# Row tiles 4 to 7 of an attention output projection in Strassen's form, in a gated attention and token-mixing kernel

## The chip, the cores and the metric

The kernel runs on one core of a Trainium2 chip. The metric is the time of one execution in device microseconds (us). The engines are TensorE (PE in the profile; PEld is its weight load), VectorE (DVE), ScalarE (ACT), GpSimd (POOL) and SyncE (SP), which only issues transfers. Each engine runs its own instructions in their order and waits for others through semaphores.

## What is computed

```python
x = A_x                                              # (1, 2048, 640), 32 heads of 20
g = sigmoid((x * gate_w).sum(-1, keepdims=True))
qkv = (x @ wqkv).reshape(B, S, 3, H, Dh)             # to q, k, v of (B, H, S, Dh)
p = softmax(einsum("bhqd,bhkd->bhqk", q, k) * Dh ** -0.5)
a = einsum("bhqk,bhkd->bhqd", p, v) -> (B, S, D) @ wo
h = layernorm(x);  u = gelu(einsum("bsd,sf->bdf", h, w1) + b1)
b = transpose(einsum("bdf,fs->bds", u, w2) + b2)
out = g * a + (1 - g) * b
```

All of it is float32. The change touches only the last product, `@ wo`, and the steps that prepare its operands.

## The kernel before

The order of every engine's instructions is the order of the code. First come the q, k and v projections and the token MLP, whose gated result is left in DRAM (`y_d`). Then a loop over 16 pairs of heads (p = 0 to 15, 32 steps each) does scores, exponentials (ACT) and the product with v (PE, `pv_flush`), and for later pairs the row maxima (DVE). `pv_evac` (L1036) copies each result from PSUM and stores the unnormalised rows of the output in `o_d` and the softmax denominators in `l_d`. The denominators of heads 0 to 27 are inverted inside the loop and stored in `r_d`. Those of the last four heads come only after the loop: `last_load` (L1019, tile `rl_last`), `last_recip` (L1025, on DVE, then a store to `rc_d` by ACT's queue), and `l_rest` (L1146), which reads `rc_d` back spread over rows.

**The projection at the end.** The attention output is transposed: 640 channels in five chunks of 128 rows, 2048 positions. Chunks 0 to 3 are loaded in eight groups of 256 positions (`e_load`, tiles `ore` for the values and `rbe` for the inverse denominators, two buffers of each); chunk 4, which holds the last heads, in four groups of 512 (`l_load`, `l_rest`, tiles `orl` and `rbl`). A group is multiplied and split in two: a high part in the fast float32 format of PE and the remainder (`o_high`, L1109, and `o_low`, L1119; `ohe`, `ole`, `ohl`, `oll`). Groups 0 to 2 of the chunks 0 to 3 are done by POOL in the last pair of the loop; the others by DVE (multiply, subtract) and ACT (copy) while the projection runs.

A row tile is 128 positions by 640 outputs, computed in two halves of 320 columns. Each product of two split operands takes three matmuls (high by high, high by low, low by high):

```python
        passes = []
        for k in cs:
            (oh, ol), n, i = (o_hl[t // 2], 2, k) if k < NC - 1 else (l_hl[t // 4], 4, 0)
            cc = slice((t % n) * P, (t % n + 1) * P)
            passes += [(oh[:, i, cc], woh[k]), (oh[:, i, cc], wol[k]), (ol[:, i, cc], woh[k])]
        mms = [(i, c) for i in range(len(passes)) for c in halves]
```

So chunks 0 to 3 of a tile cost 4 x 3 x 2 = 24 matmuls of 128x320 (`a_tile`, L1263), and chunk 4 costs 6. Tile 0 and half of tile 1 are computed inside the last pair of the loop; the other half of tile 1 follows the loop, then tiles 2 to 7 with chunks 0 to 3, and then tiles 8 to 15 with all five chunks, each followed by chunk 4 of the tile eight below it (loop at L1317). PSUM banks go round in the order `two`, `one1`/`one0`, `s`, `s3`/`pv`. The evacuation (L1290) is one DVE instruction per half: it scales by the gate and adds to the tile `oy`, loaded from `y_d` by `y_load`; it then holds the output.

Transfers of SP and ACT share eight numbered semaphores, taken in turn: a transfer is issued only after the earlier one of the same number has landed.

Of the kernel before, what the change touches and what calls it, by code (L numbers as in the profile page):

```python
# [24 lines left out]
HALF = D // 2  # L25
# [6 lines left out]
def gated_mix(ctx, tc, xT, x, wqk, wv0, wv1, wo, w1, w1t, b1, w2, b2, out):  # L32
    nc = tc.nc
# [735 lines left out]
    evacs = []  # L769
# [323 lines left out]
    tys = {}  # L1093
# [28 lines left out]
    def e_load(q):  # L1122
        o_load(q, slice(0, (NC - 1) * P), NC - 1, 256, "e", 2)

    def e_high(q, pool, eng=nc.scalar):
        o_hl[q] = o_high(q, NC - 1, 256, "e", 2, pool, eng)

    def e_low(q, eng=nc.vector):
        o_low(q, "e", o_hl[q], eng)

    L0 = (H - LAST) * DH - (NC - 1) * P

    l_raw = []

    def l_tiles():
        l_raw[:] = [ap.tile([P, 4, 512], F32, name=f"{n}l") for n in ("or", "rb")]
        for q in range(4):
            o_raw[q, "l"] = [t[:, q:q + 1] for t in l_raw]

    def l_load(q):  # L1140
        r0 = (NC - 1) * P
# [6 lines left out]
        nc.scalar.dma_start(l_raw[1][L0:, q], src)  # L1148

    def l_high(q):  # L1150
        l_hl[q] = o_high(q, 1, 512, "l", 4, ap, nc.scalar)

    def l_low(q):
        o_low(q, "l", l_hl[q], nc.vector)
# [58 lines left out]
    for p in range(NP):  # L1213
        qs = st_src[p][1]
        if 8 <= p < 8 + NC:
            load_wo(p - 8)
        for it in range(32):
            qh, kt = divmod(it, NT)
            if p + 1 < NP:
                if it == 6:  # L1220
                    st_src[p + 1] = base_stack(p + 1, True)
                if it == 13:
                    load_v(p + 1)
                if it == 27:
                    load_m(p + 1, st_src[p + 1][1], 0)
            if it == 12 and p:
                load_m(p, qs, 1)
            if it == 14 and due_stack:
                n = due_stack.pop()
                if n < NP:  # L1230
                    s_src[n] = s_stack(n)
            if p == NP - 1:
                if it in (0, 14, 18, 29):
                    e_load((0, 14, 18, 29).index(it))
                if 13 <= it < 13 + NT:
                    y_load(it - 13)
                if it in (5, 20, 25):
                    q = (5, 20, 25).index(it)
                    e_high(q, lp if q == 2 else ap, nc.gpsimd)
                    e_low(q, nc.gpsimd)  # L1240
            if kt == 0:
                pv = psum.tile([P, 512], F32, tag="pv", bufs=1, name=f"pv{p}_{qh}")
            take = min(LEFT - given, 2) if p or it > 1 else 0
            g = p * 32 + it
            if g:
                st_pair(g)
                if p == NP - 1:
                    first_row(it)
                st_one(g, 0)
            else:  # L1250
                pts[0] = first_p
            for _ in range(take):
                s_next()
            if g:
                st_one(g, 1)
            given += take
            if take and given == LEFT:
                s_finish()
            pv_flush()
            if p * 32 + it in later:  # L1260
                later.pop(p * 32 + it)()
            pend.append((p, qh, kt, pv, pts.pop(p * 32 + it)))
    def a_tile(t, cs, halves=(0, 1)):  # L1263
        n = a_count[0] % 4
        a_count[0] += 1
        name = f"a{t}_{cs[0]}"
        if n == 0:
            two = psum.tile([P, 2, 512], F32, tag="two", bufs=1, name=name)
            ps = [two[:, i, :HALF] for i in range(2)]
        elif n == 2:  # L1270
            ps = [s_tile([P, HALF], f"{name}_{i}") for i in range(2)]
        else:
            ps = [psum.tile([P, HALF], F32, tag=tag, bufs=1, name=f"{name}_{tag}") for tag in (("one1", "one0") if n == 1 else ("s3", "pv"))]
# [6 lines that stand above are left out]
        if t == NT - 1:  # L1280
            mms.sort(key=lambda e: e[1])
        for i, c in mms:
            a, b = passes[i]
            nc.tensor.matmul(ps[c], a, b[:, c * HALF:(c + 1) * HALF], start=(i == 0),  # L1284
                             stop=(i == len(passes) - 1))

        def evac():
            c = slice(t, t + 1)
            for i in halves:
                nc.vector.scalar_tensor_tensor(tys[t][:, i * HALF:(i + 1) * HALF], ps[i], g_t[:, c], tys[t][:, i * HALF:(i + 1) * HALF], op0=OP.mult, op1=OP.add)  # L1290
                if t == NT - 1:
# [12 lines left out]
    pv_flush()
    e_load(4)
    l_tiles()
    e_high(3, lp)
    e_low(3)
    last_recip()
    for q in (2, 0):  # L1310
        l_load(q)
    e_load(5)
# [1 line left out]
        l_load(q)  # L1314
    for q in (2, 0, 3, 1):
        l_rest(q)
    for t in range(2, NT):  # L1317
        q = {4: 4, 7: 5, 10: 6, 12: 7}.get(t)
        late = {6: 2, 7: 0, 8: 3, 9: 1}.get(t)
        if late is not None:  # L1320
            l_high(late)
            l_low(late)
        if q:
            e_high(q, ap if q % 4 < 2 else lp)
        evacs = [(t, range(NC) if t >= NT // 2 else range(NC - 1))]
        if t >= NT // 2:
            evacs.append((t - NT // 2, [NC - 1]))
        if t == NT - 1:
            evacs.reverse()
        evacs = [a_tile(*e) for e in evacs]  # L1330
        for f in evacs:
            f()
        if q:
            e_low(q)
            if q + 2 < NT // 2:
                e_load(q + 2)
    ordered.close()
    lps.close()

# [46 lines left out]
```

## Time and profile before

| | us |
|---|---|
| three runs | 1762.29, 1760.92, 1760.52 (median 1760.92) |
| the profiled execution: its own time | 1759.53 |
| its span, first to last instruction | 1757.7 |
| busy: PE / DVE / ACT / POOL | 1750.8 / 1251.8 / 1489.7 / 682.6 |
| last matmul of the loop's last step ends; first of tile 2 starts | about 1690.6 |

The median of the runs lies 1.39 us above the profiled execution, and the time of that lies 1.83 us above its span. Times inside the trace count from the start of the span. A busy time of PE says that matmuls were in flight, and the chain of waits says whether they waited; the timeline of the last 70 us shows what each engine did there.

### The profile page before, as it was taken

To read this page: it belongs to the slowest core of one execution; us is meant where nothing else is said; L and a number is where in the kernel's file an instruction comes from. 1 tells how busy PE (TensorE), PEld (TensorE's weight loads), DVE (VectorE), ACT (ScalarE), POOL (GpSimd) and SP (SyncE) were. 2 spreads that over 40 slices of the span, in tenths; PEclk is the share of its full clock that TensorE was granted. 3 is DMA by queue.
4 is the path that set the end of the run, shared out by engine and by line. 5 is a ranking of instruction groups with operands and counts; after the bars stand their busy time and mean duration, and the time that the engine had idled before them with its cause. 6 is when DMAs were issued, how large, how long until landed. Compare 5 with 4: busy or idle time off the path is not lost.

```text
span 1757.7 us, 39430 instructions
## 1 busy us (share of the span) xinstructions
PE 1750.8 (100%) x14972; PEld 1082.7 (62%) x14972; DVE 1251.8 (71%) x2443; ACT 1489.7 (85%) x2547; POOL 682.6 (39%) x936
## 2 busy tenths in 40 slices
PE   9999999999999999999999999999999999999999
PEld 7898899999999999533333333333333333333379
DVE  6633399988999899677767776776777777767336
ACT  5444388888888886899999999999999999999941
POOL 1434587789887777111211111121322122111410
PEclk9999999999999999999999999999999999999999
DMA  9868865476675564424313224043263144301445
GB/s 328 298 231 265 281 174 157 141 191 195 188 195 150 142 195 132 106 62 107 66 38 91 48 66 98 13 104 79 46 144 71 31 101 75 72 20 44 143 145 183
DMA packets 160945, 229.39 MB, mean 131 GB/s; under 512 B 66684, under 2 KB 97292, under 8 KB 157328
## 3 DMA queue, kind: packets, MB, share of 16 engines
q1 hardware_dynamic: 142606, 199.10, 40.6%
q0 software_dynamic: 14928, 21.86, 5.2%
q10 hardware_dynamic: 3220, 5.90, 1.1%
q8 instruction: 118, 1.93, 0.5%
q14 instruction: 73, 0.60, 0.1%
HBM read 171.07 MB, written 55.36 MB: 129 GB/s over the span
## 4 chain that ended last, share of the span: by engine, by line
PE 99%; DVE 0%; DMA 0%; ACT 0%; issue 0%; SPq 0%; ACTq 0%; DVEq 0%
PE pv L1065 29%; PE st L1164 23%; PE s L213 11%; PE y L49 10%; PE u L49 10%; PE qk L55 8%; PE v L501 4%; PE a L1284 1%; PE a_one L1284 1%; PE a_pv L1284 1%; PE a_s L1284 1%; PE a L49 0%; DMA xr<-in_xT_dram 0%; DVE mx L219 0%; PE y L894 0%
## 5 line engine op out<-in xcount | busy, mean ns | idle before, releaser
L219 DVE TENSOR_REDUCE mx<-s 128x1 f32<-128x512 f32 x1280 | 835.2, 687 | 281.8 <-PE s L213 147.0
L1182 ACT ACTIVATE p<-st 128x512 f32<-128x512 f32 x1022 | 560.5, 612 | 0.0
L1065 PE MATMUL pv<-p,v 128*32 128x512 f32 x4088 | 544.5, 605 | 0.0
L1171 ACT ACTIVATE p<-st 128x1024 f32<-128x1024 f32 x511 | 529.8, 1037 | 1.2 <-PE st L1164 1.1
L1164 PEld LDWEIGHTS st<-qs_True,ks_True 62*128 62x128 f32 x2044 | 243.8, 185 | 432.9 <-ACT p L1171 426.8
L1164 PE MATMUL st<-qs_True,ks_True 62*128 62x512 f32 x2044 | 494.0, 445 | 0.0
L213 PE MATMUL s<-ks_False,qs_False 60*128 60x512 f32 x1152 | 318.5, 391 | 0.3 <-ACT p L1182 0.2
L44 POOL TENSOR_TENSOR wl<-wr,wh 128x512 fp32r<-128x512 f32 x228 | 275.3, 1218 | 61.9 <-ACT wh L41 48.8
L238 DVE CUSTOM_DVE_ANT_0 ov<-s,ov 128x512 f32<-128x512 f32 x384 | 264.0, 688 | 36.5 <-PE s L213 25.2
L228 ACT ACTIVATE ov<-s 128x512 f32<-128x512 f32 x384 | 228.8, 598 | 62.4 <-PE s L213 54.3
L213 PE MATMUL s<-sk,sq 60*128 60x512 f32 x896 | 281.4, 394 | 0.0
L1046 POOL DMA_DIRECT2D l_d<-oev x124 | 60.4, 494 | 390.5 <-DVE oev L1038 387.8
L49 PE MATMUL y<-gh,wh 64*128 64x320 f32 x896 | 198.1, 305 | 0.0
L1065 PEld LDWEIGHTS pv<-p,v 128*32 128x32 f32 x4088 | 80.5, 108 | 187.0 <-issue 175.3
L49 PE MATMUL y<-gh,wl 64*128 64x320 f32 x832 | 191.6, 305 | 0.0
L49 PE MATMUL y<-gl,wh 64*128 64x320 f32 x832 | 191.5, 305 | 0.0
L213 PEld LDWEIGHTS s<-ks_False,qs_False 60*128 60x128 f32 x1152 | 189.0, 184 | 2.9 <-ACT p L1182 0.7
L49 PE MATMUL u<-hh,wh 64*128 64x320 f32 x864 | 186.0, 304 | 0.0
L49 PE MATMUL u<-hl,wh 64*128 64x320 f32 x864 | 185.9, 304 | 0.0
L41 ACT ACTIVATE wh<-wr 128x512 fp32r<-128x512 f32 (+3 forms) x247 | 146.8, 598 | 41.6 <-DMA wr<-in_wqk_dram 15.5
L213 PEld LDWEIGHTS s<-sk,sq 60*128 60x128 f32 x896 | 166.2, 186 | 14.9
L49 PE MATMUL u<-hh,wl 64*128 64x320 f32 x800 | 174.6, 305 | 0.0
(217 smaller groups left out, 2424.2 us busy)
## 6 DMA issues: line engine op xcount, KB each, us to landing
wr<-in_w_dram SPq DMA_DIRECT2D x192, 256.0 KB
ks_True<-k_d SPq DMA_DIRECT2D x96, 160.0 KB
qs_True<-q_d SPq DMA_DIRECT2D x192, 80.0 KB
qs_False<-q_d SPq DMA_DIRECT2D x96, 80.0 KB
v_d<-vt SPq DMA_DIRECT2D x32, 212.0 KB
sk<-k_d SPq DMA_DIRECT2D x42, 160.0 KB
sq<-q_d SPq DMA_DIRECT2D x84, 80.0 KB
v<-v_d SPq DMA_DIRECT2D x15, 424.0 KB
```

Source lines behind the costliest of these rows:

```text
L41: nc.scalar.activation(hi, src, AF.Copy)
L44: (lo_eng or nc.vector).tensor_sub(lo, src, hi.bitcast(F32))
L49: nc.tensor.matmul(ps[k], a[r], b[r], start=start, stop=stop)
L55: nc.tensor.matmul(ps, a, b, start=(i == 0 and k == 0), stop=(i == n - 1 and k == 2))
L213: nc.tensor.matmul(ps, qs[half][r, t * P:(t + 1) * P], ks[r, kc * 512:(kc + 1) * 512], start=True, stop=True)
L219: nc.vector.tensor_reduce(mx[:, slot, j, t: t + 1], ps, axis=AX.X, op=OP.max)
L228: nc.scalar.activation(over[j, kc], ps, AF.Relu)
L238: nc.vector.tensor_tensor_reduce(ov, ps, ov, 1.0, -3.0e38, OP.add, OP.max, mx[:, slot, j, t: t + 1])
L1065: nc.tensor.matmul(pv[r: r + 32, :], v_tiles[p][:, kt, VW * j: VW * j + 32], pt[j, c], start=(kt == 0), stop=(kt == NT - 1))
L1164: nc.tensor.matmul(ps, ks[r, kt * P:(kt + 1) * P], qs[qh][r, c * 512:(c + 1) * 512], start=True, stop=True)
L1171: nc.scalar.activation(pt, ps, AF.Exp, scale=SCALE)
L1182: nc.scalar.activation(pt, ps, AF.Exp, scale=SCALE)
```

## The change

Row tiles 4 and 5 (group 2) and row tiles 6 and 7 (group 3) become two "pairs". For a pair and chunks 0 to 3 the product is a 2x2 block product: two tiles by two pairs of chunks, times two pairs of chunks by two halves of the columns. Strassen's form (Winograd's variant) takes 7 block products in place of 8. It needs four sums of blocks of the rows (T1 to T4, `t_sums`, then split by `t_high`, `t_low`) and four of blocks of `wo` (`wo_sum`). A product that belongs to several outputs is accumulated in one bank: bank X takes a first product, is evacuated to one half tile, takes the next product on top, is evacuated to another, and so on, four times in all; Y and Z are the other two banks. Each pair has 7 evacuations where two plain tiles had 4.

```diff
+    def t_sums(q):
+        raw, rb = o_keep[q]
+        r11, r12, r21, r22 = (raw[:, 2 * k: 2 * k + 2, n * P:(n + 1) * P] for k in range(2) for n in range(2))
+        t = [rb[:, j].rearrange("p (k s) -> p k s", k=2) for j in range(4)]
+        nc.gpsimd.tensor_sub(t[T1], r12, r11)
+        nc.gpsimd.tensor_sub(t[T2], r22, t[T1])
+        nc.gpsimd.tensor_sub(t[T3], r22, r12)
+        nc.gpsimd.tensor_sub(t[T4], r21, t[T2])
...
+    def wo_load():
+        for i, t in enumerate(l_raw):
+            nc.gpsimd.dma_start(wo_raw[i], wo[2 * i * P: 2 * (i + 1) * P, :].rearrange("(c p) m -> p c m", p=P))
...
+    def wo_sum(n):
...
+        nc.gpsimd.tensor_tensor(dst, a, b, op=op)
...
+        hi_lo(hi, lo, dst, hi_eng=nc.gpsimd, lo_eng=nc.gpsimd)
...
+            if p == NP - 2 and it == 8:
+                wo_load()
+            if p == NP - 2 and it in (16, 20, 24):
+                wo_sum((it - 16) // 4)
             if p == NP - 1:
-                if it in (0, 14, 18, 29):
-                    e_load((0, 14, 18, 29).index(it))
+                if it == 11:
+                    wo_sum(3)
+                if it in (0, 14, 18, 23):
+                    e_load((0, 14, 18, 23).index(it))
...
-                if it in (5, 20, 25):
+                if it in (5, 20, 25, 27):
...
                     e_low(q, nc.gpsimd)
+                    if q >= 2:
+                        t_sums(q)
...
+    def pair(q, fill):
+        t0, t1 = 2 * q, 2 * q + 1
+        X, Y, Z = o_ps[q] = [o_bank(q, k) for k in range(3)]
+        v_mm(X, [(o_x(q, 0, k), o_w(0, k)) for k in range(2)], True)
+        ev(t0, 0, X)
+        v_mm(Y, [(o_x(q, 0, 2 + k), o_w(0, 2 + k)) for k in range(2)], True)
+        ev(t0, 0, Y)
+        fill[0]()
+        v_mm(X, [(o_t(q, T2, k), o_s(2, k)) for k in range(2)], False)
+        ev(t1, 0, X)
+        fill[1]()
+        v_mm(Z, [(o_t(q, T1, k), o_s(1, k)) for k in range(2)], True)
+        ev(t1, 1, Z)
+        v_mm(X, [(o_t(q, T3, k), o_s(3, k)) for k in range(2)], False)
+        ev(t1, 1, X)
...
+    def e_pool(q):
+        raw, rb = o_raw[q, "e"]
+        oh, ol = o_hl[q] = o_tiles(q, NC - 1, 256, "e", 2, ("oh", "ol"), ap if q % 4 < 2 else lp, F32R)
+        nc.gpsimd.tensor_mul(raw, raw, rb)
+        nc.scalar.activation(oh, raw, AF.Copy)
+        nc.gpsimd.tensor_sub(ol, raw, oh.bitcast(F32))
+
+    t_high(2, nc.gpsimd)
+    t_low(2, nc.gpsimd)
     first = a_tile(1, range(NC - 1), (1,))
...
+    t_high(3, nc.scalar)
     e_load(4)
-    l_tiles()
-    e_high(3, lp)
-    e_low(3)
     last_recip()
+    t_low(3, nc.vector)
...
-    for t in range(2, NT):
...
+    e_pool(4)
+    a_tile(2, range(NC - 1))()
+
+    def third(h):
+        a_count[0] = 2 - 2 * h
+        a_tile(3, range(NC - 1), (h,))()
+
+    pair(2, [lambda: third(0), lambda: third(1)])
+    pair(3, [lambda: foot(2, 0), lambda: foot(2, 1)])
+    e_pool(5)
+    for q in (6, 7):
+        e_load(q)
+    l_high(2)
+    l_low(2)
...
+        if t == NT // 2:
+            tile8 = a_tile(*evacs[0])
+            l_high(0)
+            foot(3, 0)
+            foot(3, 1)
+            l_low(0)
+            tile8()
+            a_count[0] = 3
+            evacs = evacs[1:]
```

`v_mm` (L498) issues the same three matmuls per product. `foot` computes and evacuates the last two products of a pair (6 matmuls each). The two halves of tile 3 and the two feet of the first pair stand between products of a pair. The whole program has 12924 matmul instructions before and 12912 after.

On DVE, right after the loop (`oev` is the last copy of the loop, `oT` the low part of the sums of group 3, `a_0_one` tile 2, `o_0` bank X of the first pair, `o_1` its Y), before:

```order
L1038 COPY oev_1_26581<-pv_1_26184 128x512
L1112 TENSOR_TENSOR ore_26494<-ore_26494,rbe_26495 128x1024
L1120 TENSOR_TENSOR ole_26600<-ore_26494,ohe_26599 128x1024
L1026 RECIPROCAL rl_last<-rl_last 128x64
L1290 SCALAR_TENSOR_TENSOR oy_26113<-a_0_one_26622,g_t,oy_26113 128x320
L1290 SCALAR_TENSOR_TENSOR oy_26113<-a_0_one_26623,g_t,oy_26113 128x320
```

and now:

```order
L1038 COPY oev_1_26618<-pv_1_26203 128x512
L1026 RECIPROCAL rl_last<-rl_last 128x64
L1153 TENSOR_TENSOR oT<-rbe_26379,oT 128x1024
L1348 SCALAR_TENSOR_TENSOR oy_26132<-a_0_one_26659,g_t,oy_26132 128x320
L1348 SCALAR_TENSOR_TENSOR oy_26132<-a_0_one_26660,g_t,oy_26132 128x320
L1364 SCALAR_TENSOR_TENSOR oy_26201<-o_0_26687,g_t,oy_26201 128x320
L1364 SCALAR_TENSOR_TENSOR oy_26201<-o_1_26688,g_t,oy_26201 128x320
```

The multiply and subtract of group 3 are gone from here; the reciprocal stands first, a subtract of the same size follows it, and the first evacuation of bank X is five instructions behind the copy.

On PE, the second product into bank X (`o_0`, with the sums `oTh` and `oTl`) now comes straight after the first half of tile 3 (`a_0_0`):

```order
L1342 MATMUL a_0_0_26704<-wol_13608,ohe_26306 128x320
L1342 MATMUL a_0_0_26704<-woh_13603,ole_26307 128x320
L501 MATMUL o_0_26687<-wsum,oTh 128x320 x2
L501 MATMUL o_0_26687<-wsum,oTl 128x320
L501 MATMUL o_0_26687<-wsum,oTh 128x320 x2
L501 MATMUL o_0_26687<-wsum,oTl 128x320
L1342 MATMUL a_0_26726<-woh_13600,ohe_26306 128x320
```

The first product into `o_0` stands 24 matmuls earlier than the second; the copy of `o_0` by DVE has to come between them.

On DVE where tile 8 is computed (`orl`, `ohl`, `oll` are chunk 4; `o_0` and `o_2` here are banks X and Z of the second pair's feet, `a_0 ... x2` is tile 8, `a_4_s` chunk 4 of tile 0), now:

```order
L1197 TENSOR_TENSOR orl<-orl,rbl 128x512
L1120 TENSOR_TENSOR oll_26820<-orl,ohl_26819 128x512
L1197 TENSOR_TENSOR orl<-orl,rbl 128x512
L1364 SCALAR_TENSOR_TENSOR oy_26281<-o_0_26754,g_t,oy_26281 128x320
L1364 SCALAR_TENSOR_TENSOR oy_26304<-o_2_26756,g_t,oy_26304 128x320
L1120 TENSOR_TENSOR oll_26856<-orl,ohl_26855 128x512
L1348 SCALAR_TENSOR_TENSOR oy_26332<-a_0_26824,g_t,oy_26332 128x320 x2
L1348 SCALAR_TENSOR_TENSOR oy_26132<-a_4_s_26877,g_t,oy_26132 128x320
```

Before, both parts of chunk 4 stood several evacuations earlier, ahead of the evacuation of tile 8; now its second low part stands behind the evacuations of both feet and ahead of that of tile 8.

## Rows read from the trace of the kernel before

**Rows 1.** Page, the chain that ended last: shares by engine.
```profile
PE 99%; DVE 0%; DMA 0%; ACT 0%; issue 0%; SPq 0%; ACTq 0%; DVEq 0%
```
**Rows 2.** Windows, L1284 alone: stretch, PE busy, PE and PEld instructions, granted clock, DMA, GB/s.
```profile
1690.58:1754.04 63.46, 63.46 (x432) 63.36 (x432) 1.00 0.55 184
```
**Rows 3.** Timeline of PE: start us, us, engine line, out<-in, count.
```profile
1690.58 0.56 PE L1284 MATMUL a_one<-woh,ohe 128*128 128x320 f32 x2
...
1697.72 0.31 PE L1284 MATMUL a_s<-woh,ohe 128*128 128x320 f32 x1
...
1717.08 0.46 PE L1284 MATMUL a_one<-woh,ohe 128*128 128x320 f32 x2
```
**Rows 4.** Timeline of DVE after the loop; in brackets its idle time before.
```profile
1697.34 0.55 DVE L1026 RECIPROCAL rl_last<-rl_last 128x64 f32<-128x64 f32 x1 [2.42 <-DMA rl_last<-l_d]
1697.81 0.91 DVE L1290 SCALAR_TENSOR_TENSOR oy<-a_one,g_t,oy 128x320 f32<-128x320 f32 x2
...
1701.79 1.22 DVE L1112 TENSOR_TENSOR ore<-ore,rbe 128x1024 f32<-128x1024 f32 x1 [2.15 <-DMA rbe<-r_d]
1702.93 0.54 DVE L1290 SCALAR_TENSOR_TENSOR oy<-a_s,g_t,oy 128x320 f32<-128x320 f32 x1
...
1707.59 1.23 DVE L1120 TENSOR_TENSOR ole<-ore,ohe 128x1024 fp32r<-128x1024 f32 x1 [3.65 <-ACT ohe L1114]
1708.73 1.00 DVE L1290 SCALAR_TENSOR_TENSOR oy<-a,g_t,oy 128x320 f32<-128x320 f32 x2
1710.16 0.69 DVE L1112 TENSOR_TENSOR orl<-orl,rbl 128x512 f32<-128x512 f32 x1 [0.42 <-DMA rbe<-r_d]
...
1715.33 1.22 DVE L1112 TENSOR_TENSOR ore<-ore,rbe 128x1024 f32<-128x1024 f32 x1
```
**Rows 5.** Timeline of SP's queue after the loop: last denominators, groups 4 and 5.
```profile
1694.28 0.35 SPq L1022 DMA_DIRECT2D rl_last<-l_d  x1
...
1695.16 1.39 SPq L1091 DMA_DIRECT2D rbe<-r_d  x1
...
1704.14 0.50 SPq L1091 DMA_DIRECT2D rbe<-r_d  x1
```
**Rows 6.** Timeline of ACT after the loop.
```profile
1706.50 1.06 ACT L1114 ACTIVATE ohe<-ore 128x1024 fp32r<-128x1024 f32 x1 [12.84 <-DMA rbl<-rc_d]
1710.89 0.63 ACT L1114 ACTIVATE ohl<-orl 128x512 fp32r<-128x512 f32 x1 [3.33 <-DVE orl L1112]
```
**Rows 7.** Timeline of POOL: group 2 in the loop, the stores after it.
```profile
1669.78 2.39 POOL L1112 TENSOR_TENSOR ore<-ore,rbe 128x1024 f32<-128x1024 f32 x1
1672.23 1.04 POOL L1116 CAST ohe<-ore 128x1024 fp32r<-128x1024 f32 x1
1673.35 2.41 POOL L1120 TENSOR_TENSOR ole<-ore,ohe 128x1024 fp32r<-128x1024 f32 x1
...
1691.73 2.04 POOL L1049 DMA_DIRECT2D o_d<-oev  x4 [15.98 <-DVE oev L1038]
```
**Rows 8.** Timeline of POOL and DVE in the v projection, one unit.
```profile
82.37 0.75 POOL L446 TENSOR_TENSOR vr<-vx 128x256 f32<-128x256 f32 x1
82.83 1.39 DVE L44 TENSOR_TENSOR vT<-vr,vT 128x1024 fp32r<-128x1024 f32 x1 [4.37 <-ACT vT L41]
83.20 1.61 POOL L447 TENSOR_TENSOR vr<-vx,vr 128x256 f32<-128x256 f32 x1
```
**Rows 9.** Timeline of PE at the start of the program: successive warm-up matmuls.
```profile
1.44 4.01 PE L374 MATMUL warm_ps<-warm 128*128 128x512 f32 x10 [1.44 <-DVE warm L371]
...
2.89 1.05 PE L374 MATMUL warm_ps<-warm 128*128 128x512 f32 x2
3.32 1.05 PE L374 MATMUL warm_ps<-warm 128*128 128x512 f32 x2
...
4.60 0.85 PE L374 MATMUL warm_ps<-warm 128*128 128x512 f32 x3
```
**Rows 10.** Groups of instructions on POOL: a 128x640 operation, as in the sums of wo.
```profile
L44 POOL TENSOR_TENSOR wol<-wor,woh 128x640 fp32r<-128x640 f32 x5 | 7.8, 1567 | 0.4
```

More of the change, by code (lines that the diff above doesn't have):

```diff
@@ L1131, in gated_mix @@
     L0 = (H - LAST) * DH - (NC - 1) * P
[L1133 to L1138, printed above, removed]
+    o_keep, t_tiles, t_hl = {}, [], {}
+    def t_sums(q):
[6 more added lines that the diff above has]
+        nc.gpsimd.tensor_sub(t[T4], r21, t[T2])
@@ new lines, in t_high, with t_low @@
+    def t_high(q, eng):
+        raw, rb = o_keep[q]
+        t_hl[q] = t_tiles[q % 2]
+        if eng is nc.scalar:
+            nc.scalar.activation(t_hl[q][0], rb, AF.Copy)
+        else:
+            eng.tensor_copy(t_hl[q][0], rb)
+    def t_low(q, eng):
+        raw, rb = o_keep.pop(q)
+        eng.tensor_sub(t_hl[q][1], rb, t_hl[q][0].bitcast(F32))
+    l_raw = [ap.tile([P, 4, 512], F32, name=f"{n}l") for n in ("or", "rb")]
+    for q in range(4):
+        o_raw[q, "l"] = [t[:, q:q + 1] for t in l_raw]
@@ new lines, in gated_mix @@
+    w_rows = ap.tile([P, 12, HALF], F32R, name="wsum")
+    w_sums = {}
+    def wo_load():
+        for i, t in enumerate(l_raw):
+            nc.gpsimd.dma_start(wo_raw[i], wo[2 * i * P: 2 * (i + 1) * P, :].rearrange("(c p) m -> p c m", p=P))
+    flat = [t.rearrange("p a b -> p (a b)") for t in l_raw]
+    wo_raw = [f[:, :2 * D].rearrange("p (c m) -> p c m", c=2) for f in flat]
+    w_s1 = flat[0][:, 2 * D: 3 * D].rearrange("p (c m) -> p c m", c=2)
+    def wo_sum(n):
+        (a11, a21), (a12, a22) = ((r[:, :, :HALF], r[:, :, HALF:]) for r in wo_raw)
+        dst, a, b, op = ((w_s1, a21, a22, OP.add), (a21, a11, a21, OP.subtract), (w_s1, w_s1, a11, OP.subtract),
+                         (a12, a12, w_s1, OP.subtract))[n]
+        nc.gpsimd.tensor_tensor(dst, a, b, op=op)
+        if n < 3:
+            hi, lo = w_rows[:, 4 * n: 4 * n + 2], w_rows[:, 4 * n + 2: 4 * n + 4]
+        else:
+            hi = ap.tile([P, 2, HALF], F32R, tag="wor", bufs=1, name="wsum4h")
+            lo = base.tile([P, 2, HALF], F32R, tag="v", bufs=1, name="wsum4l")
+        hi_lo(hi, lo, dst, hi_eng=nc.gpsimd, lo_eng=nc.gpsimd)
+        w_sums[(1, 3, 2, 4)[n]] = hi, lo
@@ L1150, in l_high @@
     def l_high(q):
-        l_hl[q] = o_high(q, 1, 512, "l", 4, ap, nc.scalar)
+        tiles = [lp.tile([P, 1, 512], F32R, tag="pt", bufs=5, name=f"{n}l{q}") if 2 * q + i < 5 else
+                 lp.tile([P, 1, 512], F32R, tag="pp", bufs=3, name=f"{n}l{q}") for i, n in enumerate(("oh", "ol"))]
+        raw, rb = o_raw[q, "l"]
+        nc.vector.tensor_mul(raw, raw, rb)
+        nc.scalar.activation(tiles[0], raw, AF.Copy)
+        l_hl[q] = tiles
     def l_low(q):
@@ L1231, in gated_mix @@
                     s_src[n] = s_stack(n)
+            if p == NP - 2 and it == 8:
+                wo_load()
+            if p == NP - 2 and it in (16, 20, 24):
+                wo_sum((it - 16) // 4)
             if p == NP - 1:
-                if it in (0, 14, 18, 29):
-                    e_load((0, 14, 18, 29).index(it))
+                if it == 11:
+                    wo_sum(3)
+                if it in (0, 14, 18, 23):
+                    e_load((0, 14, 18, 23).index(it))
                 if 13 <= it < 13 + NT:
                     y_load(it - 13)
-                if it in (5, 20, 25):
-                    q = (5, 20, 25).index(it)
-                    e_high(q, lp if q == 2 else ap, nc.gpsimd)
+                if it in (5, 20, 25, 27):
+                    q = (5, 20, 25, 27).index(it)
+                    e_high(q, lp if q >= 2 else ap, nc.gpsimd)
+                    if q >= 2:
+                        o_keep[q] = o_raw[q, "e"]
                     e_low(q, nc.gpsimd)
+                    if q >= 2:
+                        t_sums(q)
             if kt == 0:
@@ L1299, in gated_mix, with ev, o_x, o_t @@
     a_count = [0]
+    t_tiles[:] = [[q4([P, 4, 256], F32R, f"oT{n}") for n in "hl"]]
+    both_t = k8([P, 2, 4, 256], F32R, "oT")
+    t_tiles.append([both_t[:, i] for i in range(2)])
+    def ev(t, i, ps):
+        cols = slice(i * HALF, (i + 1) * HALF)
+        nc.vector.scalar_tensor_tensor(tys[t][:, cols], ps, g_t[:, t:t + 1], tys[t][:, cols], op0=OP.mult, op1=OP.add)
+    def o_x(q, n, c):
+        return [e[:, c, n * P:(n + 1) * P] for e in o_hl[q]]
+    def o_t(q, j, k):
+        return [e[:, j, k * P:(k + 1) * P] for e in t_hl[q]]
+    def o_w(i, c):
+        return [e[c][:, i * HALF:(i + 1) * HALF] for e in (woh, wol)]
+    def o_s(j, k):
+        return [e[:, k] for e in w_sums[j]]
+    o_ps = {}
+    def o_bank(q, k):
+        tag = (("s3", "pv", "one0"), ("one1", "s", "s"))[q % 2][k]
+        return psum.tile([P, HALF], F32, tag=tag, bufs=2 if tag == "s" else 1, name=f"o{q}_{k}")
+    def pair(q, fill):
[13 more added lines that the diff above has]
+        ev(t1, 1, X)
+    def foot(q, k):
+        t0, t1 = 2 * q, 2 * q + 1
+        X, Y, Z = o_ps[q]
+        if k == 0:
+            v_mm(X, [(o_t(q, T4, k), o_w(1, 2 + k)) for k in range(2)], False)
+            ev(t0, 1, X)
+        else:
+            v_mm(Z, [(o_x(q, 1, 2 + k), o_s(4, k)) for k in range(2)], False)
+            ev(t1, 0, Z)
+            t_hl.pop(q)
+    def e_pool(q):
[4 more added lines that the diff above has]
+        nc.gpsimd.tensor_sub(ol, raw, oh.bitcast(F32))
     assert not row_mms
+    t_high(2, nc.gpsimd)
+    t_low(2, nc.gpsimd)
     first = a_tile(1, range(NC - 1), (1,))
@@ L1316, in gated_mix @@
         l_rest(q)
-    for t in range(2, NT):
[L1318 to L1322, printed above, removed]
-        if q:
[L1324 to L1327, printed above, removed]
+    e_pool(4)
[10 more added lines that the diff above has]
+    l_low(2)
+    a_count[0] = 0
+    for t in range(NT // 2, NT):
+        q = {10: 6, 12: 7}.get(t)
+        if q:
+            e_high(q, lp)
+        evacs = [(t, range(NC)), (t - NT // 2, [NC - 1])]
+        if t == NT // 2:
[7 more added lines that the diff above has]
+            evacs = evacs[1:]
         if t == NT - 1:
@@ L1334, in gated_mix @@
             e_low(q)
-            if q + 2 < NT // 2:
-                e_load(q + 2)
+        if t in (9, 10):
+            l_high((3, 1)[t - 9])
+            l_low((3, 1)[t - 9])
     ordered.close()
```

## The prediction

> **What bounds the kernel now.** I read four views, in this order. The chain that ended last gives PE 99% [rows 1], so a saving counts only if it is PE's, and any new wait of PE counts in full. The windows show PE after the loop: 432 matmuls of 128x320, in flight without a gap for 63.46 us, which is 0.147 us each [rows 2]. The timeline of PE gives the starts that I count from: the first matmul of tile 2, the first of tile 4 (48 matmuls later) and tile 9 [rows 3]. The timelines of DVE, SP, ACT and POOL show what each does beside that [rows 4 to 8]. DVE idles for 2.42 us ahead of the reciprocal of the last denominators, which land only at 1697.34. Before, PE did not feel it: it was computing tiles 2 and 3.
>
> **What is removed.** A plain pair takes 8 block products of 6 matmuls, a Strassen pair 7. Two pairs save 12 matmuls: 12 x 0.147 = **1.76 us** [rows 2]. Rows and columns keep their sizes, so I price the new products alike. This is all that can be won.
>
> **Wait 1: the second product into bank X of the first pair.** PE comes to it after 24 matmuls of tile 2, 12 into X and Y, and 12 of tile 3. That is 48, as many as stood before the first of tile 4, so without a wait it would start at 1697.72 [rows 3]. But bank X must be copied out first, and that copy is five instructions behind the loop's last copy on DVE, which takes its order as it is written. The denominators don't come sooner: their load is issued at 1694.28 as before, since nothing that the change moves stands ahead of it on SP [rows 5]. So DVE starts the reciprocal at 1697.34 and the subtract of group 3's sums 0.47 later, at 1697.81 [rows 4]. Such a subtract, 128x1024, takes 1.14 to the next start (1707.59 to 1708.73): 1698.95. Two evacuations of tile 2 take 0.45 each (1.00 for two that overlap, less 0.54 for one, both in rows 4): 1699.85. The evacuation of X takes 0.55: 1700.40. PE waits 1700.40 - 1697.72 = **2.7 us**. Then T2, the other half of tile 3, Z and T3 are 30 matmuls, 4.4 us, to 1704.8. The second pair with the first pair's feet is 42, 6.2 us, to 1711.0. Its evacuations have DVE to themselves.
>
> **Wait 2: chunk 4 of tile 8.** Tile 8's other chunks take 24 matmuls, 1711.0 to 1714.5, and need the split rows of group 4. ACT copies them at 1706.50 to 1707.56, held by the transfers of the last denominators as before [rows 6], and POOL subtracts in 2.4 [rows 7], to 1710.0: in time. Chunk 4 has a new queue. POOL multiplies group 5 when its denominators have landed, near 1710.1 by the row that waits for them [rows 4], to 1712.5. ACT copies in 1.06, to 1713.6, and only then, as its order is written, the 0.63 of `ohl` [rows 6], to 1714.2. DVE subtracts in 0.69, to 1714.9. PE asks for it after 28 matmuls, at 1715.1, so this fits by 0.2 us. One thing spoils it: POOL's multiply runs beside a multiply of chunk 4 on DVE. Where a POOL operation of 128x256 ran beside a DVE operation with two operands in SBUF, it took 1.61 in place of 0.75 [rows 8]. A stretch of about 0.6, since the DVE one lasts 0.69 [rows 4], makes the wait **0.5 us** (bounds 0 and 0.9, the whole stretch of 0.86 above the 0.2 of room).
>
> **Waits 3 and 4: tile 8 to tile 9.** Chunk 4 of tile 0 needs its low part, which on DVE now stands behind the evacuations of both feet of the second pair. Let the last foot's matmuls end at T. Its evacuation starts then, the subtract 0.45 later, and that ends 0.69 later, at T + 1.14. PE has 4 matmuls that don't need it, 0.59: a wait of 0.55 as laid out, 1.14 if these hide nothing. I take **0.8 us**, since both ends of PE's matmuls are modelled. Tile 9 takes the bank of tile 8, whose two evacuations start 0.61 behind that subtract's start (0.69 less 0.08, by which successive instructions of DVE overlap: 1.22 from 1701.79 reaches past 1702.93) and take 1.00 [rows 4]: T + 2.06. PE ends the last 2 matmuls of chunk 4 at T + 1.14 + 0.29 = T + 1.43: **0.65 us**. Both could be 0 if DVE runs further ahead; below 0 they can't be, since before PE had no gap. Tile 9 would start at about 1720.0 against 1717.08 [rows 3].
>
> **What I put at nothing, and its cover.** The sums of `wo` on POOL take two instructions of 1.57 each [rows 10] and a cast, four times, in pairs 14 and 15, where PE goes on with scores and the stores queued behind them on POOL belong to heads read a pair later. In the last pair POOL has, from group 2's start at 1669.78, 5.9 for that group [rows 7], 3.0 for four sums of 0.75 [rows 8], the same 8.9 for group 3, and 3.5 for splitting the first pair's sums: 1691.1. PE wants these at 1697.7. If the stretch of rows 8 hits all eight sums (8 x 0.86 = 6.9), this room of 6.6 is just spent, and it would show inside wait 1, which has 2.7 of its own. The stores of the last head, at 1691.73 behind that [rows 7], may be late by the same, but SP's queue has slack behind them until 1704 [rows 5]. Group 3 is loaded earlier and its multiply leaves DVE; DVE is not what ends there.
>
> **Sum.** -1.76 + 2.7 + 0.5 + 0.8 + 0.65 = **+2.9 us**. The profiled execution took 1759.53, so it becomes 1762.4. The median of the runs, 1760.92, is 1.39 above it; I add the 2.9 to the median: **1763.8 us**. A measurement of this kernel can tell about 0.2%, 3.5 us, from no change: the edges are 1757.4 and 1764.4. So the forecast is no change that can be told, from the slow side of it.
>
> **Rivals.** *The first wait doesn't come.* It would take denominators that land 2.7 us earlier; the idle time ahead of the reciprocal says that DVE would use that at once. The load of group 5 would have to come as much earlier, for chunk 4 hangs on its landing: if wait 1 alone shrank, wait 2 would grow by the same. Against it: both loads keep their place in SP's order [rows 5]. Then the sum is -1.76 + 0.5 + 0.8 + 0.65 = +0.2, 1761.1; with the later waits gone too, the floor is -1.76, 1759.2. Chance 0.17.
>
> *The sixth group comes late* (this ends on the other side, slower by over 0.2%). Chunk 4 stands on ACT behind the copy of group 5, that behind POOL's multiply, and that behind the load of its denominators. Group 4's load was issued at 1695.16 [rows 5] and released DVE at 1701.79 [rows 4], 6.6 later. The same from 1704.14 [rows 5] gives 1710.7, not 1710.1, and every delay past 1710.1 is PE's in full. By 1710.7 the total is +3.5, the edge: from there on this mechanism decides. A delay of twice that, 1.2, gives +4.1, 1765.0. The trace of before can't exclude it, since DVE used that load only at 1715.33 [rows 4]; for a landing so late the price would be 5.2. For it speaks that the row naming that load as releaser may have waited for another; against it, that the same row is the only direct sight of it. Chance 0.15.
>
> *The clock of PE falls after the first wait.* [...] In the tail the granted clock is 1.00 [rows 2], and the trace of before has no wait of 2.7 us behind which to see it fall. If it fell, 320 columns would be 0.43 x 320/512 = 0.269 us apart in place of 0.147; from the first matmul, at 1.44, to 4.60 are 3.16 us [rows 9]. In so long a time 11.7 matmuls would be done in place of 21.5; what is lost is 3.16 x (1 - 0.147/0.269) = 1.4 us. The sum is then +4.3, 1765.2. [...] Since the wait is shorter than all that the engine did before it, I give it 0.10.
>
> **How the numbers follow.** The forecast keeps 0.58. Its unknown terms (the stretch of 0 to 0.9, wait 3 of 0 to 1.14, wait 4) and the spread of the three runs put it past 1764.4 in about 0.13 of the 0.58. Slower: 0.13 + 0.15 + 0.10 = 0.38. Faster needs more than the 1.76 that is removed, which only the measurement could give: 0.02. The same: 0.60. The range goes from the floor, 1759.2, which takes in the first rival, to 1766.0, which takes in the other two with 0.8 for a later landing; some 0.15 lies outside.
>
> **What would show it.** Right: PE idle for about 2.7 us up to 1700.4, ahead of a product of bank X and released by DVE's evacuation, with the reciprocal at 1697.3 and the subtract of the sums between; 420 matmuls after the loop; short waits of PE for the low parts of chunk 4 and for the bank of tile 8; tile 9 at 1719.5 to 1720.0; POOL's multiply of group 5 longer than 2.4; granted clock 1.00. Wrong: no idle time near 1698; matmuls 0.27 apart after it; group 5's multiply starting past 1710.7; or a wait anywhere inside the loop, which would mean that POOL's work there is not covered.

## The result: slower, and the profile after

The changed kernel takes 1770.26 us (median of 6 runs, 1769.04 to 1773.14) against 1761.58 of the kernel before in the same set (6 runs, 1760.52 to 1764.52): a ratio of 1.0049, 95% interval 1.0036 to 1.0062. That is 8.7 us more, where +2.9 was predicted, and outside the range.

The two profiles differ by 10.6 us in span (1768.3 and 1757.7), but not all of that is the change. By source line, the copies that end each half pair of the loop (32 of them, L1038) give their first and last start, of the kernel after:

```profile
L1038 DVE COPY oev<-pv x32: 690/692/693, 749.8 to 1692.7; 128x512 f32<-128x512 f32 x32
```

Before, they went from 747.8 to 1690.7. The 2.0 us are there at the first copy, some 825 us ahead of the first new instruction (1575, the load of `wo`), and stay 2.0 to the last: nothing that POOL now does in the last two pairs adds to the time of the loop. What is left happens behind the loop. The windows of that stretch, from its first matmul to the end, before and then after (stretch, its length, then busy time and instructions of PE, PEld, DVE, ACT, POOL, the granted clock, DMA share, GB/s):

```profile
1690.58:1757.70 67.12, 63.62 (x436) 63.36 (x432) 39.15 (x64) 7.83 (x9) 2.04 (x4) 1.00 0.53 177
```
```profile
1692.55:1768.30 75.75, 64.58 (x424) 63.04 (x420) 38.70 (x65) 7.72 (x9) 11.85 (x9) 0.98 0.47 156
```

12 weight loads fewer, as said; PE is not busy for 11.2 us where it was for 3.5; the granted clock is no longer 1.00; the stretch is 8.63 us longer. This stretch is the measure used below, since it leaves out what the start of the program adds from one execution to the next.

PE had no wait behind the loop before [rows 2]. Now its waits are (us in total, times, longest us):

```profile
PE a L1342 <- ACT ohl L1198: 2.7, 1, 2.7
...
PE o L501 <- DVE oy L1364: 2.4, 1, 2.4
PE a L1342 <- DVE oll L1120: 1.6, 1, 1.6
...
PE a_s L1342 <- DVE oll L1120: 0.7, 1, 0.7
PE a L1342 <- DVE oy L1348: 0.4, 1, 0.4
```

The timeline of PE gives them their places:

```profile
1699.55 0.31 PE L1342 MATMUL a<-woh,ole 128*128 128x320 f32 x1
1702.26 0.53 PE L501 MATMUL o<-wsum,oTh 128*128 128x320 f32 x2 [2.40 <-DVE oy L1364]
...
1716.10 0.46 PE L1342 MATMUL a<-woh,ole 128*128 128x320 f32 x2
1719.26 0.56 PE L1342 MATMUL a<-woh,ohl 128*128 128x320 f32 x2 [2.71 <-ACT ohl L1198]
1719.66 0.45 PE L1342 MATMUL a<-wol,ohl 128*128 128x320 f32 x2
1721.73 0.90 PE L1342 MATMUL a<-woh,oll 128*128 128x320 f32 x2 [1.62 <-DVE oll L1120]
1722.43 0.47 PE L501 MATMUL o<-woh,oT 128*128 128x320 f32 x1
...
1725.34 0.30 PE L1342 MATMUL a_s<-woh,ohl 128*128 128x320 f32 x1
...
1726.74 0.42 PE L1342 MATMUL a_s<-woh,oll 128*128 128x320 f32 x1 [0.66 <-DVE oll L1120]
...
1727.66 0.56 PE L1342 MATMUL a<-woh,ohe 128*128 128x320 f32 x2 [0.36 <-DVE oy L1348]
```

The numbers in brackets begin at modelled ends, so I count from start to start, less the 0.147 that each matmul takes [rows 2]: 2.56 ahead of T2; 2.87 ahead of the high part of chunk 4; 1.78 ahead of its low part; 0.82 and 0.52 at tile 0's chunk 4 and tile 9. From 1721.73 to 1725.34 are 14 matmuls, 2.05 at 0.147 each, and they took 3.61: 1.56 more. The first matmuls after each wait are spread a little, 0.39 together. The sum, 10.50, less 1.76 for the 12 matmuls is 8.74, against 8.63 measured.

The windows say what the slow matmuls are (columns as above):

```profile
1721.70:1723.00 1.30, 1.27 (x5) 1.27 (x6) 0.58 (x1) 0.63 (x1) 0.00 (x0) 0.50 0.67 194
1723.00:1724.00 1.00, 1.00 (x5) 1.00 (x5) 0.00 (x0) 0.00 (x0) 0.00 (x0) 0.50 1.08 373
```

The granted clock is 0.50 behind the two waits around chunk 4, where matmuls start 0.27 us apart (1722.43 and 1722.69).

And the other engines, in one list by time, from the timelines of SP, DVE, POOL and ACT:

```profile
1705.86 0.45 SPq L1091 DMA_DIRECT2D rbe<-r_d  x1
...
1713.55 0.68 DVE L1197 TENSOR_TENSOR orl<-orl,rbl 128x512 f32<-128x512 f32 x1
...
1715.24 2.37 POOL L1414 TENSOR_TENSOR ore<-ore,rbe 128x1024 f32<-128x1024 f32 x1 [3.44 <-DMA rbe<-r_d]
...
1717.63 1.06 ACT L1415 ACTIVATE ohe<-ore 128x1024 fp32r<-128x1024 f32 x1 [8.30 <-POOL ore L1414]
1718.60 0.61 ACT L1198 ACTIVATE ohl<-orl 128x512 fp32r<-128x512 f32 x1
...
1718.77 2.36 POOL L1416 TENSOR_TENSOR ole<-ore,ohe 128x1024 fp32r<-128x1024 f32 x1 [1.17 <-ACT ohe L1415]
...
1719.24 2.43 DVE L1120 TENSOR_TENSOR oll<-orl,ohl 128x512 fp32r<-128x512 f32 x1 [5.01 <-ACT ohl L1198]
```

Read it as a chain. Chunk 4 was multiplied at 1713.55 and ready for its copy at 1714.2. ACT sat idle for 8.30 us and would not take it, since group 5's copy stands ahead. That one waits for POOL, and POOL for the denominators, which released it 9.4 us after their issue. Then DVE's subtract takes 2.43, where an operation of this size takes 0.69 in [rows 4]: it ends at 1721.67, 0.54 behind the end of POOL's subtract (1721.13), though POOL's took no longer than alone (2.41 in [rows 7]). In this trace POOL had started 0.47 us earlier (1718.77 and 1719.24), and DVE paid.

### The profile page after: what moved, and what is told of

Same layout as the page of the kernel before. It is cut to its first block, busy times and chain, and to the rows that moved or that the text cites. A ratio compares the mean times of both kernels' runs of the same rounds, so it can differ in the third digit from the quotient of the medians.

```text
span 1768.3 us, 39456 instructions
## 1 busy us (share of the span) xinstructions
PE 1752.3 (99%) x14960; PEld 1082.4 (61%) x14960; DVE 1251.1 (71%) x2444; ACT 1489.3 (84%) x2547; POOL 723.0 (41%) x967
```

## The experiments

My theory after this: the Strassen products cost what plain ones do, and all the loss is order. A wait on DVE behind the denominators (wait 1); chunk 4 behind group 5 on ACT, with POOL in DVE's way (wait 2); the two short waits; and a clock that falls with idle time. The rivals were that chunk 4's own rows come late, that the Strassen form or POOL's sums cost time of their own, and that the clock is taken for another reason.

| kernel | runs, us (before in the same set) | ratio, 95% interval | stretch after the loop, over before's 67.12 |
|---|---|---|---|
| the change | 1770.26 (1761.58) | 1.0049, 1.0036 to 1.0062 | +8.63 |
| chunk 4 ahead of group 5 | 1766.59 (1761.32) | 1.0030, 1.0020 to 1.0040 | +6.19 |
| group 5 on DVE | 1765.16 (1761.32) | 1.0019, 1.0009 to 1.0028 | +3.56 |
| X first | 1770.99 (1761.32) | 1.0055, 1.0038 to 1.0072 | +8.67 |
| waits at chunk 4 filled | 1769.89 (1761.32) | 1.0047, 1.0032 to 1.0061 | +7.35 |
| group 5 loaded earlier | 1765.89 (1761.58) | 1.0029, 1.0018 to 1.0040 | +3.90 |
| all waits taken away | 1759.91 (1761.58) | 0.9990, 0.9981 to 0.9999 | -1.82 |
| before, group 5's multiply on POOL | 1764.1 (1761.64), one run | none | +0.05 |
| group 5 on DVE, first wait filled | 1763.77 (1761.64) | 1.0022, 1.0002 to 1.0043 | +2.31 |

The stretch is the span less the start of the first matmul behind the loop, in the one profiled execution of each. A ratio compares a kernel with the kernel before, run beside it.

**Chunk 4 ahead of group 5.**

```diff
+    l_high(2)
+    l_low(2)
     e_pool(5)
     for q in (6, 7):
         e_load(q)
-    l_high(2)
-    l_low(2)
```

> The multiply, copy and subtract of chunk 4 for tile 8 are written ahead of group 5's; nothing else moves. In the profile of the change PE lost 2.87 us ahead of the high part of chunk 4, 1.78 ahead of its low part and some 1.55 by the half clock that followed. Theory (chunk 4 stood on ACT behind group 5, whose denominators landed late): all three go, 6.2 us. But POOL's two long operations of group 5 now stand in the way of chunk 4 of tile 0 on DVE, which I put at about +1.2, so the tile 9 starts some 30.1 us after tile 2 (the change 35.1, before 26.5), and the time is about 3.7 us over the kernel before. Rival (chunk 4's own rows land late, group 5 only came at the same time): the wait ahead of chunk 4 stays, 8 us or more over before.

Both waits at tile 8 are gone, and tile 9 starts 30.07 us after tile 2 (1722.36 less 1692.29), as expected:

```profile
1722.36 0.90 PE L1342 MATMUL a<-woh,ohe 128*128 128x320 f32 x2
```

So chunk 4's own rows were there in time. POOL's group 5 now holds up the chunk 4 of tile 0 on DVE, twice, as timelines of DVE and POOL show:

```profile
1714.96 2.88 DVE L1197 TENSOR_TENSOR orl<-orl,rbl 128x512 f32<-128x512 f32 x1
1719.07 2.32 DVE L1120 TENSOR_TENSOR oll<-orl,ohl 128x512 fp32r<-128x512 f32 x1
...
1714.62 2.68 POOL L1414 TENSOR_TENSOR ore<-ore,rbe 128x1024 f32<-128x1024 f32 x1 [3.39 <-DMA rbe<-r_d]
...
1718.47 2.36 POOL L1416 TENSOR_TENSOR ole<-ore,ohe 128x1024 fp32r<-128x1024 f32 x1 [1.17 <-ACT ohe L1415]
```

Up to there the loss over before is 3.57 us (30.07 less 26.50); at the end it is 6.19. The other 2.6 are the clock: behind the wait of 1.61 that the second of these causes it fell, and for longer than in the change. Windows of that kernel:

```profile
1721.40:1724.00 2.60, 2.54 (x8) 2.15 (x9) 1.82 (x4) 0.00 (x0) 0.00 (x0) 0.50 0.84 253
1724.00:1728.00 4.00, 4.00 (x17) 4.00 (x16) 0.00 (x0) 0.00 (x0) 0.00 (x0) 0.50 0.86 263
```

I had left the clock out of that sum.

**Group 5 on DVE.** Its multiply and subtract go to DVE, behind tile 8's evacuation (with group 7's load behind them):

```diff
-    e_pool(5)
-    for q in (6, 7):
-        e_load(q)
+    e_load(6)
...
             evacs = evacs[1:]
+            e_high(5, ap)
...
+        if t == NT // 2:
+            e_low(5)
+            e_load(7)
```

> Group 5 is multiplied and subtracted by DVE as in the kernel before, after tile 8's evacuation; POOL has only group 4. Theory (late landing of group 5 and DVE's subtract blocked by POOL's): the wait ahead of chunk 4, the 2.43 us of its subtract (0.69 expected) and the half clock go, and nothing of POOL stands in the way of tile 0's chunk 4. Waits of about 0.6 each for its low part and for the bank of tile 8 stay. Tile 9 starts about 28.5 us after tile 2 and the time is about 2.0 over before. Rival (the loss hangs on the Strassen products or on the evacuations): 6 us or more over before.

No wait is left at tile 8, its subtract takes 0.69, and the two short waits stay:

```profile
1721.07 0.41 PE L1342 MATMUL a_s<-woh,oll 128*128 128x320 f32 x1 [0.66 <-DVE oll L1120]
...
1721.99 0.56 PE L1342 MATMUL a<-woh,ohe 128*128 128x320 f32 x2 [0.36 <-DVE oy L1348]
```

Tile 9 starts 29.97 us after tile 2 (1692.02), not 28.5: this time the clock fell behind the *first* wait. Windows:

```profile
1701.30:1702.30 1.00, 0.94 (x5) 0.97 (x6) 0.98 (x2) 0.00 (x0) 0.07 (x1) 0.76 0.79 210
1702.30:1703.30 1.00, 1.00 (x6) 1.00 (x5) 0.38 (x2) 0.00 (x0) 1.00 (x1) 0.50 1.04 342
1703.30:1704.30 1.00, 1.00 (x5) 1.00 (x5) 0.20 (x1) 0.00 (x0) 1.00 (x1) 0.50 0.48 147
```

From 1701.73 to 1705.32 were 14 matmuls: 3.59 in place of 2.05, 1.54 lost. Without it tile 9 would have come 28.43 after tile 2.

**X first.** The first product into X is computed ahead of tile 2 and evacuated ahead of the reciprocal:

```diff
+    def pair_x(q):
+        X = o_bank(q, 0)
+        o_ps[q] = [X]
+        v_mm(X, [(o_x(q, 0, k), o_w(0, k)) for k in range(2)], True)
+        ev(2 * q, 0, X)
...
     e_load(4)
+    pair_x(2)
     last_recip()
     t_low(3, nc.vector)
```

> The first product into bank X of the first pair is computed ahead of tile 2 and evacuated on DVE ahead of the reciprocal of the last denominators. Theory: the wait of 2.56 us ahead of the second product into X goes (0 to 0.3 us left), but chunk 4 of tile 8 becomes ready at the same time as in the change, so tile 8 waits about 1 us for group 4's low part and chunk 4 waits the rest longer: tile 9 starts 34.6 to 35.6 us after tile 2's stretch began (the change 35.1), and the time stays 8 to 9.5 us over before. Rival (the waits are independent): 2.5 us less than the change, 6 over before.

Wait 1 is gone and the stretch is no shorter, +8.67 against +8.63. The waits of PE there:

```profile
PE a L1342 <- ACT ohl L1198: 4.2, 1, 4.2
...
PE a L1342 <- DVE oll L1120: 1.0, 1, 1.0
PE a L1342 <- POOL ole L1424: 0.6, 1, 0.6
```

What wait 1 gave back went to group 4's low part (0.6) and to chunk 4 (4.2 in place of 2.7). The waits are one chain with its end fixed by a landing: what is taken from one goes to the next. That the two stretches agree to 0.04 us is partly luck. The low part of chunk 4 started 0.39 us sooner after the first matmul than in the change (28.79 and 29.18), and the clock, low for longer (0.50 over all of 1720 to 1725), took as much back. Two rows of this kernel, of DVE and of POOL, show more:

```profile
1711.52 0.69 DVE L1197 TENSOR_TENSOR orl<-orl,rbl 128x512 f32<-128x512 f32 x1 [0.48 <-DMA rbe<-r_d]
...
1714.94 2.34 POOL L1422 TENSOR_TENSOR ore<-ore,rbe 128x1024 f32<-128x1024 f32 x1 [3.40 <-DMA rbe<-r_d]
```

Both name the same transfer as their releaser, 3.4 us apart. Only POOL's reads `rbe`.

**The waits at chunk 4 filled** with matmuls whose result nobody reads:

```diff
+        if t == NT // 2:
+            spare = psum.tile([P, HALF], F32, tag="one0", bufs=1, name="spare")
         for i, c in mms:
+            if t == NT // 2 and c == 0 and i in (12, 14):
+                for _ in range(16 if i == 12 else 9):
+                    nc.tensor.matmul(spare, passes[0][0], passes[0][1][:, :HALF], start=True, stop=True)
```

> 16 and 9 matmuls of 128x320 whose result nobody reads are put into the two waits of PE ahead of chunk 4 of tile 8 (2.87 and 1.78 us long; they take 2.35 and 1.32). No wait gets shorter by itself. Theory (the clock fell because PE stood idle in these two waits): the granted clock stays 1.00 from 1721 on, the 12 products behind them go at 0.147 us each and not 0.27, and the time is 1.4 to 1.7 us under the change, some 7.2 over before. Rival (the clock was taken for another reason, or needs the first wait as well): no difference from the change, the clock still at half.

The stretch is 1.28 us shorter than the change's, and the clock stayed up where it had fallen. Windows of the same place:

```profile
1715.00:1720.00 5.00, 5.00 (x36) 5.00 (x36) 3.90 (x2) 1.58 (x2) 3.83 (x2) 1.00 0.85 262
1720.00:1725.00 5.00, 4.64 (x32) 4.38 (x30) 3.19 (x5) 0.63 (x1) 0.58 (x1) 1.00 0.85 259
```

The DMA share is 0.85 in both, against 0.73 and 0.93 in the same two windows of the change, which speaks for PE's idle time, and not for the transfers, as what takes the clock; one execution can't show it, as the fall did not come each time. The runs, 8.6 over before, can't tell the 1.3 us. In this execution, too, the clock fell behind the first wait, which was not filled; that cost nothing at the end, for the reason of the experiment above.

**Group 5 loaded earlier**, ahead of chunk 4's first two loads:

```diff
+    e_load(5)
     for q in (2, 0):
         l_load(q)
-    e_load(5)
```

> Group 5 is loaded ahead of the two loads of chunk 4 that stood before it on SP; nothing else moves. In the change its denominators were issued at 1705.86 and released POOL at 1715.24, 9.4 us later. Theory (they land late because they are issued behind chunk 4's loads, and run beside the broadcast reads of the last denominators): they land by 1708, POOL is through with both groups by 1714.5, the copy of chunk 4 on ACT no longer stands behind them, and both waits ahead of chunk 4 and the half clock behind them go: tile 9 starts about 29 us after tile 2 (the change 35.1, before 26.5), 2.5 to 3 over before. Rival (the transfers share one bandwidth): chunk 4's rows come later by what group 5 gains, PE still waits over 1 us ahead of chunk 4's high part, and the time stays 5 us or more over before.

Half of it came true: the wait for the high part of chunk 4 is gone, and with it the half clock, but the stretch is 3.9 over before and not 2.5 to 3. The low part still waited 1.5 us, as these rows of DVE and POOL show:

```profile
1715.27 2.45 DVE L1120 TENSOR_TENSOR oll<-orl,ohl 128x512 fp32r<-128x512 f32 x1 [1.10 <-ACT ohl L1198]
...
1711.22 2.40 POOL L1414 TENSOR_TENSOR ore<-ore,rbe 128x1024 f32<-128x1024 f32 x1
1714.80 2.37 POOL L1416 TENSOR_TENSOR ole<-ore,ohe 128x1024 fp32r<-128x1024 f32 x1 [1.17 <-ACT ohe L1415]
```

POOL took group 5 without waiting for it, so it had landed by 1711.22, but behind its own subtract of group 4, and its last subtract again lay across DVE's.

**All waits taken away.** X first, as above; group 5 on DVE; tile 8 does its passes with the low part of group 4 last; and tile 9 is computed ahead of chunk 4 of tile 0, in other banks. The edits that are not in one of the experiments above:

```diff
+        if t == NT // 2:
+            passes[:12] = [e for i, e in enumerate(passes[:12]) if i % 3 < 2] + passes[2:12:3]
...
             l_high(0)
             foot(3, 0)
             foot(3, 1)
+            tile8()
             l_low(0)
-            tile8()
+            e_high(5, ap)
             a_count[0] = 3
-            evacs = evacs[1:]
+            continue
+        if t == NT // 2 + 1:
+            evacs.append((0, [NC - 1]))
```

> Strassen's form is kept and every wait is taken away by order: the first product into X is computed ahead of tile 2 and evacuated ahead of the reciprocal; group 5 goes back to DVE, behind tile 8; tile 8 does its passes with the low part of group 4 last; tile 9 is computed ahead of chunk 4 of tile 0. Theory (the products cost what plain matmuls of this size do, and all the loss was waits): no wait of PE over 0.2 us after the loop, granted clock 1.00, the time 1.2 to 1.8 us under before (ratio 0.9990 to 0.9993). Rival (something of the change other than its waits costs time, such as POOL's work in the loop or the seven evacuations of a pair): not under before.

1759.91 us against 1761.58, ratio 0.9990 (0.9981 to 0.9999). The profile has no wait of PE behind the loop, and the windows over the whole stretch give:

```profile
1691.90:1757.20 65.30, 61.82 (x424) 61.55 (x420) 39.06 (x67) 7.83 (x9) 7.12 (x7) 1.00 0.54 181
```

1.82 us less than before, for 12 matmuls of 0.147, 1.76. So the Strassen products cost what plain matmuls cost, and the sums on POOL and the six more evacuations cost PE nothing. This version is some 10 us faster than the change, and 1.7 us (0.1%) faster than the kernel before, by an interval that only just leaves out no difference.

**Before, group 5's multiply on POOL.** The kernel before with that one multiply moved to the idle POOL, as a probe for the landing:

```diff
-        (nc.vector if hi_eng is nc.scalar else hi_eng).tensor_mul(raw, raw, rb)
+        (mul_eng or (nc.vector if hi_eng is nc.scalar else hi_eng)).tensor_mul(raw, raw, rb)
...
+        o_hl[q] = o_high(q, NC - 1, 256, "e", 2, pool, eng, nc.gpsimd if q == 5 else None)
```

> The kernel before, with one edit: the multiply of group 5 is done by POOL, which is idle there, so that the start of that multiply shows when the group's denominators land. Theory (the row of DVE that named them waited for chunk 4's own rows, as it does not read group 5 at all; the landing was always late): POOL starts some 22.2 to 22.8 us after the first matmul of tile 2, as in the four kernels with the change, while DVE's first multiply of chunk 4 starts at 19 to 20 us, again with the denominators of group 5 named as its releaser. PE still has no wait. Rival (in the kernel before they did land at 19.5 us, and the change made them 3 us later): POOL starts at 19 to 20 us.

The first matmul of tile 2 starts at 1695.03 there. DVE and POOL:

```profile
1714.49 0.69 DVE L1112 TENSOR_TENSOR orl<-orl,rbl 128x512 f32<-128x512 f32 x1 [0.33 <-DMA rbl<-rc_d]
...
1718.12 2.42 POOL L1112 TENSOR_TENSOR ore<-ore,rbe 128x1024 f32<-128x1024 f32 x1 [19.91 <-DMA rbe<-r_d]
```

POOL starts 23.09 us after tile 2, a little over the expected range, and DVE's multiply of chunk 4 at 19.46. So the denominators of group 5 land late without the change too; PE didn't feel it, because nothing needed them yet. The releaser's name came out otherwise than I expected: this time the row names `rbl`, which it does read.

How late they were in the profiled execution of the kernel before needs no second execution. The kept trace has the times at which this load's semaphore was updated: 16 updates, from 1708.85 to 1712.33, the last 21.75 us after tile 2. In the change it stands at 1715.10 (22.55), 0.14 ahead of POOL's start, and in the probe at 1717.96 (22.93). In the eight kernels besides the change that issue this load at its old place, the kernel before among them, it lies between 20.29 and 23.14. The semaphores also say why the row in [rows 4] had the wrong name: one of those that it waits for is that of chunk 4's load of 1697.15, and group 5's load of 1704.14 counts on the same one.

**Group 5 on DVE, first wait filled** with 13 such matmuls:

```diff
         fill[0]()
+        if q == 2:
+            spare = psum.tile([P, 2, 512], F32, tag="two", bufs=1, name="spare")
+            for _ in range(13):
+                nc.tensor.matmul(spare[:, 0, :HALF], *[e[0] for e in (o_x(q, 0, 0), o_w(0, 0))], start=True, stop=True)
```

> As the kernel with group 5 on DVE, with 13 matmuls whose result nobody reads put into the first wait of PE (1.91 us of some 2.3). Theory (the half clock seen there after the first wait comes from PE standing idle and is had in some executions only): granted clock 1.00 over the whole stretch after the loop, the stretch from tile 2 to the end 1.8 to 2.2 us over before where the profile without the filling had 3.6, and the median of the runs 0.5 to 1.6 us under that kernel's. Rival (the fall has another cause): half clock again for 3 us or more.

The clock holds over the whole stretch:

```profile
1692.97:1762.40 69.43, 64.49 (x437) 63.47 (x433) 39.33 (x67) 7.83 (x9) 7.12 (x7) 1.00 0.50 171
```

The stretch is 1.25 us shorter than without the filling (+2.31, where 1.8 to 2.2 was expected), and the median 2.1 over its before where that kernel's was 3.8 over. The intervals overlap, so the medians alone would not settle it. The clock does, and not in one execution only: the mean granted clock of the whole program is 1.000 in 8 of these 10 runs, and in 2 of the 10 without the filling; one fall as above makes it 0.999. Of the other two runs here one has 0.999, and one, 1779.45 us long, has 0.949.

## Why the prediction was wrong

**Removed: right.** 12 matmuls, 1.76 us; 1.82 where nothing else is in the way.

**Wait 1: right.** Forecast 2.7, measured 2.56, at the place and by the chain described: the reciprocal, the subtract of the sums, two evacuations, X. The work on POOL that I put at nothing cost nothing.

**Wait 2: this step failed.** Forecast 0.5, measured 4.65 (2.87 and 1.78). Its start was "POOL multiplies group 5 when its denominators have landed, near 1710.1 by the row that waits for them [rows 4]". That row is `orl<-orl,rbl`: it reads chunk 4, not group 5, and can't have waited for `rbe`, whatever the bracket says. By the semaphore they landed at 1712.33 in that execution, 2.2 later. In the change POOL started 22.69 us after tile 2, which is 1713.3 in the times of the kernel before, 3.2 later than I had it; the last 0.9 of that is more than the trace of before could tell. The only row of before that does read that load was DVE's at 1715.33, without a wait: all it gave was an upper bound, and the landing was 3.0 below it and 2.2 above my value. The rival of the late sixth group had this mechanism, the same doubt about the row, and 5.2 us as its price at the bound; I gave it 0.15 and priced it at 1.2 us late.

The second half of wait 2 was wrong in its direction. From [rows 8] I let DVE stretch POOL by 0.6; here POOL started first and DVE was stretched by 1.74. The rows had shown one order of two. Together: 3.2 for the landing and 1.74 for DVE, less the room of 0.2 that I had found, make 4.7, against 4.65.

**Waits 3 and 4:** forecast 0.8 and 0.65, measured 0.82 and 0.52.

**The clock: a rival that came true at another place.** I put its fall behind wait 1, at 1.4 us and 0.10. The 1.4 was an estimate: the 0.43 between the starts of 2.89 and 3.32 in [rows 9], taken over the time up to 4.60. No run shows that those starts were at a lower clock: in the trace of before the record of the granted clock begins at 4.59. What the runs show: in the change's profile it fell at wait 2, to 0.50 for 3.41 us (1721.56 to 1724.97), and cost 1.56; in two of the other kernels it did fall behind wait 1 and cost 1.54 in the one counted. The price was near that of these two falls, but under the 2.6 with chunk 4 first; the chance was too low; and it was a price for each wait, not for one.

**The remark that waits 1 and 2 trade against each other was right:** the experiment with X first bore it out. It means that the sum holds only as it stands, each wait counted behind the one before, and that no term of it says what would be won by removing that wait. As it stands it holds: 2.9, with 4.7 for wait 2 in place of 0.5 and 1.6 for the clock, comes to 8.7, against 8.6.

## What to carry to other kernels

Check a releaser's name against what the instruction reads: if it doesn't read the tile named, the row says nothing of when that tile arrived, and a load whose user never waits has only an upper bound. Before work is moved to another engine, ask what stands *behind* it in that engine's order (here ACT's copy of chunk 4, needed sooner than the copy ahead of it: its rows were ready at 1714.2, and it started at 1718.60). Where several waits hang on one arrival, removing one of them can only move the time to the next (here 2.56 us of wait 1, with the stretch at +8.67 against +8.63). And count with a lower clock behind each wait of PE like those here: it did not come each time, and the falls counted cost 1.54 to 2.6 us.

## What was not expected of the hardware

The clock fell after waits shorter than I thought mattered, and not each time. Idle time of 2.03 us ahead of T2 was followed by a granted clock of 0.50 in one kernel, and 2.40 us at the same place in the change was not; 1.61 us at tile 0 was followed by it in the kernel with chunk 4 first. In the kernel with filled waits it fell only 1.3 us after PE had begun again. The falls counted here cost between 1.54 and 2.6 us each. What decides it in a single wait stays open.

Open too is why the denominators of group 5 take so long. From issue to the last update of the semaphore they took 9.2 us in the change and 7.4 to 10.5 in the other kernels that issue them at the same place, where group 4's took 4.4 to 6.5. They run beside the reads of the last denominators (in the change issued at 1705.86, and those from 1705.43 on). Issued 5.3 us earlier, counted from the end of the loop, in the kernel that loads group 5 earlier, they took 6.7 (1699.92 to 1706.65); more these runs don't tell.
